# Attention phases of 12 and 14 scores of one head, with two thirds of the q/k projection beside the first 8 groups

## The chip, the cores and the metric

The kernel runs on one core of a Trainium2 chip. The metric is the device time of one execution in microseconds (us). The core has five engines with a queue of instructions each: PE (TensorE, the matrix engine), ACT (ScalarE), DVE (VectorE), POOL (GpSimd) and SP (SyncE, which here only issues DMA transfers). They wait for each other by semaphores. PSUM, where PE writes, has 8 banks of 128 x 512 fp32.

## The reference

The inputs are fp32 with S = 2048 rows, D = 512 columns, H = 32 heads of 16, F = 1792:

```python
x = A_x
g = _sigmoid((x * gate_w).sum(-1, keepdims=True))
# attention
scores = jnp.einsum("bhqd,bhkd->bhqk", q, k) * Dh ** -0.5    # q, k, v from x @ wqkv
a = einsum(softmax(scores), v) @ wo
# token mixing
h = _layernorm(x)
u = _gelu(jnp.einsum("bsd,sf->bdf", h, w1) + b1)             # tanh form
b = (jnp.einsum("bdf,fs->bds", u, w2) + b2)                  # turned back to (b, s, d)
return g * a + (1 - g) * b
```

## The kernel before

fp32 operands are cut in two parts, hi and lo, and a product is three matmuls (hi·hi, hi·lo, lo·hi). P = 128, NB = 512, so a full matmul is 128 rows deep and 512 columns wide; `split` makes a hi part by a copy (ACT or DVE) and a lo part by a subtraction (DVE or POOL). The work is in stages, one after another on PE:

1. x is turned and cut, and v = x·wv is projected; v stays in SBUF.
2. The whole q/k projection: 32 tiles of 12 full matmuls (`products`, L91), alone on PE. Each result is cut and stored in DRAM (`kp_d`, `qp_d`).
3. The first layer (u = gelu(h·w1 + b1)): 14 blocks of 128 columns of w1, 672 full matmuls (L469), in passes of 4 blocks. After a pass `gelu` works its blocks off with ACT and DVE; the last two blocks are worked off where the attention begins.
4. The attention: 32 groups (a pair of heads and half of the queries) of 8 phases, a phase having 8 scores. A score is one matmul 64 rows deep (L926), on one half of the array; on the other half stands, at the same time, a half of a matmul that needs no attention: second layer or output projection (a "dense" matmul, L1053). A phase has 6 or 8 dense ones and scores of both heads. ACT takes the exponentials (L949): two singles of 128 x 512 and three pairs of 128 x 1024, from PSUM into tiles of the pool `pt` (7 buffers of two scores each, 4 tiles in a phase). In 24 of the groups DVE takes one pair instead, by a polynomial (L966 to L990). Behind the 8 scores stand the products with v (A·V) of the phase before (L882, `apply_v`): four matmuls of 17 columns by 256 for each score, in four column strips of the array. DVE adds their bank to the sum of the group (L902). So PE's queue is: 8 scores of phase p, A·V of phase p-1, 8 scores of phase p+1, and so on. The scores and A·V share a ring of 7 banks, by the written table `TURN`; the dense matmuls have the eighth bank.
5. The end: the last group is divided by its sums, and the remaining output matmuls, the adds and the stores of the last 8 row tiles follow.

The stages of the attention are built under a manual schedule: each engine runs its instructions in the order in which the code writes them.

Of the kernel before, what the change touches and what calls it, by code (L numbers as in the profile page):

```python
# [22 lines left out]
P = 128  # L23
# [53 lines left out]
def gated_mix(ctx: ExitStack, tc: tile.TileContext, a_x, a_wqkv, a_wo, b_w1, b_b1, b_w2, b_b2, gate_w, out):  # L77
# [21 lines left out]
    kp_d = [dram.tile([2, P, S], F32, name=f"kp{b}") for b in range(ND)]  # L99

# [13 lines left out]
    v_pool = ctx.enter_context(tc.tile_pool(name="v", bufs=1))  # L114
    v = v_pool.tile([P, NS, H, VC], F32, name="v")

    acc_ctx, wk_ctx, h_ctx, xt_ctx, u_ctx, qk_ctx = (ExitStack() for _ in range(6))
    acc = acc_ctx.enter_context(tc.tile_pool(name="acc", bufs=8, space=PSUM))
    wk = wk_ctx.enter_context(tc.tile_pool(name="wk", bufs=3, side="right"))

    def bank():
        return acc.tile([P, NB], F32, name="acc")


# [3 lines left out]


    order = {f0: [(c + (NS // 2 if f0 + NB >= F else 0)) % NS for c in range(NS)] for f0 in range(0, F, NB)}  # L130
    blocks = [b_w1[c * P : (c + 1) * P, f0 : min(f0 + NB, F)] for f0 in order for c in order[f0]]
    blocks += [
        b_w2[c * P : min(c + 4, NF) * P, t * P : (t + 1) * P].rearrange("(k p) s -> p k s", p=P)
        for t in range(NS)
        for c in range(0, NF, 4)
    ]
    loaded, ready, subs = [], [], []

    def load_weight():
        if blocks:  # L140
            src = blocks.pop(0)
            raw = wk.tile([P, NB], F32, name="w_raw", bufs=4)
            if len(src.shape) == 2:
                raw = raw[:, : src.shape[1]]
                dst = raw
            else:
                raw = raw[:, : src.shape[1] * P]
                dst = raw.rearrange("p (k s) -> p k s", s=P)
            with tc.issue_after(x_load.ins):
                nc.sync.dma_start(dst, src)  # L150
            loaded.append(raw)

    def split_weight(copy=None, sub=None):
        if loaded:
            raw = loaded.pop(0)
            hi = wk.tile([P, NB], F32R, name="w_hi")[:, : raw.shape[1]]
            lo = wk.tile([P, NB], F32R, name="w_lo")[:, : raw.shape[1]]
            subs.append(split(hi, lo, raw, copy or nc.scalar.copy, sub or nc.gpsimd.tensor_tensor))
            ready.append((hi, lo))

    def weight():
        load_weight()
        split_weight()
        return ready.pop(0)
# [14 lines left out]

    def wcols(c0):  # L180
        with tc.issue_after(x_load.ins):
            loaded = load_wcols(c0)
        return split_wcols(*loaded)
# [5 lines left out]
    with tc.tile_pool(name="vp", bufs=1, side="right") as pool:  # L189
# [70 lines left out]

        def v_out(t, ps):
            nc.scalar.copy(v[:, t, :, 0:DH], ps.rearrange("p (h d) -> p h d", d=DH))

        with tc.manual_schedule():
# [64 lines left out]
            for t in range(2, NS):  # L329
# [19 lines left out]
                ps = bank()  # L349
# [4 lines left out]
        pool.tile([P, 40], F32, name="pad")  # L354
        e = pool.tile([P, NS], F32, name="e")
        nc.scalar.activation(e, z, AF.Exp, scale=-1.0)
        nc.vector.tensor_scalar_add(e, e, 1.0)
        nc.vector.reciprocal(g, e)
        nc.vector.tensor_scalar(omg, g, -0.5, 0.5, ALU.mult, ALU.add)
        y, t, w = (pool.tile([P, NS], F32, name=n) for n in "ytw")  # L360
        nc.vector.tensor_scalar_add(w, mv[:, :, 1], EPS)
        nc.scalar.activation(y, w, AF.Sqrt)
        nc.vector.reciprocal(y, y)

        nc.vector.tensor_mul(t, y, y)
        nc.vector.tensor_mul(t, t, w)
        nc.vector.tensor_scalar(t, t, -0.5, 1.5, ALU.mult, ALU.add)
        nc.vector.tensor_mul(rs, y, t)


    NH = NS // 2
    h_hi, h_lo = {}, {}
    AHEAD = 3

    def h_half(lo):
        h_pool = h_ctx.enter_context(tc.tile_pool(name=f"h{lo}", bufs=1))
        hi_t = h_pool.tile([P, NH, D], F32R, name="h_hi")
        lo_t = h_pool.tile([P, NH, D], F32R, name="h_lo")
        for i in range(NH):
            h_hi[lo + i], h_lo[lo + i] = hi_t[:, i, :], lo_t[:, i, :]  # L380

    def ln_load(ln, c, bufs=3):
        xs[c] = ln.tile([P, D], F32, name="x", bufs=bufs)
        nc.sync.dma_start(xs[c], xf[c * P : (c + 1) * P, :])

    def ln_rows(ln, c):
        hf = ln.tile([P, D], F32, name="hf", bufs=2)
        nc.vector.tensor_scalar(hf, xs[c], mv[:, c, 0:1], rs[:, c : c + 1], ALU.subtract, ALU.mult)
        split(h_hi[c], h_lo[c], hf, nc.scalar.copy, nc.vector.tensor_tensor)


    h_half(0)
    bd = h_ctx.enter_context(tc.tile_pool(name="bd", bufs=2))
    bd.tile([P, 56], F32, name="pad", bufs=1)
    with tc.tile_pool(name="ln0", bufs=3, side="right") as ln:

        def project(w, n):
            ps = bank()
            cols = slice(n * NB, (n + 1) * NB)
            hi, lo = w  # L400
            products(ps, [((hi[:, k, :], lo[:, k, :]), (xt_hi[:, k, cols], xt_lo[:, k, cols])) for k in range(ND)])
            return ps
# [837 lines left out]
```

## Time and profile before

| | |
|---|---|
| times of 3 runs | 1267.86, 1268.37, 1269.83 us |
| median | 1268.37 us |
| span of the profiled execution | 1268.3 us |
| busy PE, ACT, DVE, POOL | 99%, 84%, 58%, 18% of the span |
| v and what is ahead of it | 0 to about 50 us |
| q/k projection | about 50 to 139.6 us |
| first layer | 139.6 to 292.1 us |
| attention | 292.1 to 1251.3 us |
| end | 1251.3 to 1268.3 us |

The profiled execution's span is within 0.1 us of the median, so the two are used as one. The busy time of PE is not its useful time: matmuls are pipelined, and a matmul that waits for its turn in the array counts. In rows of the timeline the columns are start and duration in us, engine, line, operation, output <- inputs, shapes, and the count of like instructions that the row takes together. A row of grouped instructions has the count, then the summed time in us and the mean in ns, then the idle time ahead and what ended it.

### The profile page before, as it was taken

The page shows a single profiled execution, that of the slowest core. Times are in us where ns is not written, and L with a number is a line of the kernel's source. Part 1 is how long each engine was busy: PE and PEld are TensorE (multiplying, and loading weights), DVE is VectorE, ACT ScalarE, POOL GpSimd, SP SyncE. Part 2 cuts the span into 40 slices and gives each one's busy share as a digit, 9 for nine tenths or more (in the row PEclk, how much of TensorE's full clock was granted, in tenths as well). Part 3 has the DMA queues.
Part 4 walks back from the last instruction along what each step waited for, and adds up shares of the span by engine and source line. Part 5 has one row for each costly group of instructions (what it writes and reads, how often), then busy time and mean ns, then how long its engine had stood idle before and what let it go on. Part 6 is the DMA issues. An engine that isn't in the chain of part 4 may idle for free.

```text
span 1268.3 us, 33491 instructions
## 1 busy us (share of the span) xinstructions
PE 1259.9 (99%) x13230; PEld 795.6 (63%) x13230; DVE 732.1 (58%) x1342; ACT 1070.1 (84%) x1481; POOL 228.3 (18%) x447
## 2 busy tenths in 40 slices
PE   9999999999999999999999999999999999999998
PEld 7888888886555555555555555555555555555555
DVE  6775362536677666666747656666665662325425
ACT  4444343438999999999999999999999999999994
POOL 4510244553111111111110011111111111100000
PEclk9999999999999999999999999999999999999999
DMA  6787644324223232222444432222222234336622
GB/s 188 218 295 295 226 131 131 98 75 129 73 77 77 75 87 71 77 66 77 128 100 115 117 82 70 69 73 77 76 78 67 77 83 104 95 99 189 156 61 70
DMA packets 108037, 141.10 MB, mean 111 GB/s; under 512 B 20265, under 2 KB 65599, under 8 KB 107872
## 3 DMA queue, kind: packets, MB, share of 16 engines
q1 hardware_dynamic: 107440, 138.09, 38.2%
q8 instruction: 107, 1.75, 0.6%
q10 hardware_dynamic: 432, 0.79, 0.2%
q14 instruction: 58, 0.48, 0.1%
HBM read 102.64 MB, written 36.16 MB: 109 GB/s over the span
## 4 chain that ended last, share of the span: by engine, by line
PE 98%; DMA 0%; DVE 0%; ACT 0%; SPq 0%; issue 0%; ACTq 0%
PE s L882 38%; PE s L926 34%; PE acc L469 12%; PE acc L91 10%; PE dn L1053 4%; PE pa L1124 1%; DMA x<-in_A_x_dram 0%; PE acc L299 0%; PE pa L1133 0%; PE dn L912 0%; PE acc L210 0%; DVE ot L482 0%; SPq L202 0%; DVE base L1152 0%; DVE row L482 0%; ACT row L484 0%
## 5 line engine op out<-in xcount | busy, mean ns | idle before, releaser
L949 ACT ACTIVATE pt<-s 128x1024 f32<-128x1024 f32 (+1 forms) x1256 | 941.4, 945 | 10.6 <-PE s L926 4.5
L926 PE MATMUL s<-qs,ks 64*128 64x512 f32 x2048 | 493.7, 404 | 0.1
L882 PE MATMUL s<-pt,v 128*17 128x256 f32 x8000 | 481.4, 381 | 0.0
L926 PEld LDWEIGHTS s<-qs,ks 64*128 64x128 f32 x2048 | 324.0, 184 | 164.9 <-ACT pt L949 87.8
L902 DVE TENSOR_TENSOR ot<-s,ot 128x256 f32<-128x256 f32 (+2 forms) x431 | 191.5, 444 | 339.6 <-PE s L882 266.2
L882 PEld LDWEIGHTS s<-pt,v 128*17 128x17 f32 x8000 | 209.5, 97 | 233.3 <-ACT pt L949 85.6
L1053 PE MATMUL dn<-u_hi,w_hi 64*128 64x512 f32 x428 | 186.2, 435 | 0.0
L84 POOL TENSOR_TENSOR w_lo<-w_raw,w_hi 128x512 fp32r<-128x512 f32 (+1 forms) x127 | 150.5, 1187 | 170.1 <-ACT w_hi L83 103.9
L1053 PE MATMUL dn<-u_lo,w_hi 64*128 64x512 f32 x430 | 169.4, 394 | 0.0
L1053 PE MATMUL dn<-u_hi,w_lo 64*128 64x512 f32 x430 | 169.1, 393 | 0.0
L1057 POOL MEMSET token<- 1x1 f32 x256 | 25.6, 100 | 779.2 <-PE dn L1053 672.8
L83 ACT CAST w_hi<-w_raw 128x512 fp32r<-128x512 f32 (+1 forms) x67 | 37.8, 569 | 76.6 <-PE acc L469 56.6
L972 DVE SCALAR_TENSOR_TENSOR row<-row,zs 128x512 f32<-128x512 f32 x144 | 99.3, 690 | 4.1
L469 PE MATMUL acc<-h_hi,w_lo 128*128 128x512 f32 x224 | 87.2, 389 | 0.0
L469 PE MATMUL acc<-h_hi,w_hi 128*128 128x512 f32 x224 | 87.1, 389 | 0.0
L469 PE MATMUL acc<-h_lo,w_hi 128*128 128x512 f32 x224 | 87.1, 389 | 0.0
L1053 PEld LDWEIGHTS dn<-u_hi,w_lo 64*128 64x128 f32 x430 | 79.2, 184 | 1.2
L1053 PEld LDWEIGHTS dn<-u_lo,w_hi 64*128 64x128 f32 x430 | 79.4, 185 | 0.8
L1053 PEld LDWEIGHTS dn<-u_hi,w_hi 64*128 64x128 f32 x428 | 78.6, 184 | 1.3
L91 PE MATMUL acc<-xt_hi,wc_hi 128*128 128x512 f32 x128 | 49.8, 389 | 0.0
L91 PE MATMUL acc<-xt_lo,wc_hi 128*128 128x512 f32 x128 | 49.8, 389 | 0.0
L91 PE MATMUL acc<-xt_hi,wc_lo 128*128 128x512 f32 x128 | 49.8, 389 | 0.0
(164 smaller groups left out, 1185.8 us busy)
## 6 DMA issues: line engine op xcount, KB each, us to landing
w_raw<-in_B_w_dram SPq DMA_DIRECT2D x96, 256.0 KB
ks<-kp SPq DMA_DIRECT2D x384, 64.0 KB
qs<-qp SPq DMA_DIRECT2D x256, 64.0 KB
qp<-pc SPq DMA_DIRECT2D x16, 768.0 KB
x<-in_A_x_dram SPq DMA_DIRECT2D x32, 256.0 KB
kp<-pc SPq DMA_DIRECT2D x16, 512.0 KB
w_raw<-in_B_w_dram SPq DMA_DIRECT2D x32, 128.0 KB
bp<-row SPq DMA_DIRECT2D x16, 256.0 KB
```

The source lines that it names most:

```text
L83: copy(hi, src)
L84: return sub(lo, src, hi.bitcast(F32), ALU.subtract)
L91: nc.tensor.matmul(ps, a, b, start=start and n == 0, stop=stop and n == last)
L469: nc.tensor.matmul(p, a, b, start=first and k == 0, stop=last and k == 2)
L882: mm = nc.tensor.matmul(av[32 * j : 32 * j + VC, i * QC : (i + 1) * QC], v[:, c, g % NP * 2 + i, :], pt[:, h * QC : (h + 1) * QC], start=t ...
L902: reads(nc.vector.tensor_tensor(x, y, x, ALU.add), bank)
L926: mm = nc.tensor.matmul(banks[:, bank, :], kt[grp, c * P // SH][rows, c * P % SH : c * P % SH + P], qt[grp][rows, qb * NB : (qb + 1) * NB] ...
L949: act = nc.scalar.activation(dst, banks[:, at[0] : at[-1] + 1, :], AF.Exp, scale=SCALE)
L972: nc.vector.scalar_tensor_tensor(box[1], q or box[1], a, x, ALU.add, ALU.mult)
L1053: mm = nc.tensor.matmul(ps, a[half], b[half], start=first and not second, stop=last and bool(second))
L1057: fence = nc.gpsimd.memset(token, 0.0)
L1124: nc.tensor.matmul(pa[t], a, b, start=i == 0 and t not in LATE, stop=i == len(mms) - 1 and t in LATE)
```

## The change

The changed program has the stages in another order, and its attention another unit of work.

- v is stored to DRAM (`v_d`) and read back for one pair of heads at a time (`load_v`).
- 11 of the 32 tiles of the q/k projection are computed alone (`ALONE`). The other 21 (252 full matmuls) become 504 half matmuls beside the scores of the first 8 groups: pairs 0 to 3 of the heads, both halves of the queries. That is 42 phases of 12 scores, 12 dense matmuls each, and one phase of 8 scores with no dense one.
- The first layer follows, alone, in passes of 3 blocks (the last of 2). The rows of h are made in its first pass, by DVE, ACT, DVE one after another (`ln_rows`).
- The other 24 groups follow: 48 twos of phases of 14 scores (96 phases, all with the second layer beside them), then 8 twos of 12 scores (16 phases, with the output projection of the first 8 row tiles). A two is a phase of the first head of a pair and a phase of its second head with the same dense matmuls, in the two halves. Every score has a dense partner.
- DVE computes no exponential. In a phase of 14 it copies scores 1, 4 and 5 from PSUM into their places in `pt` (`park`, L559), in a phase of 12 scores 2 and 3, and ACT exponentiates these later, in place, from SBUF (L541). The order of ACT's exponentials in a phase is the list `PLANS`.
- Which bank a score gets is no table any more: `take` and `take_beside` choose while the program is built, by estimated times (`SLOT`, `PAIR`, ...). The pool `pt` has 11 buffers in the first 8 groups and 12 in the rest; a phase of 14 fills 7 of them, a phase of 12 fills 6.
- `apply_v` of the phase before still stands behind all scores of a phase, and takes the scores in the order in which their `pt` tiles were opened.
- The end has all 12 output matmuls of each of the last 8 row tiles (9 of them ahead of the last pair of heads); the odd tiles are scaled by ACT and added by POOL.

```diff
+    PLANS = {
+        14: ([(0,), (2,), (3,), (6,), (7,), (8, 9), (10, 11), (12, 13), (5,), (1, 4)], (1, 4, 5)),
+        12: ([(0,), (1,), (4,), (5,), (2, 3), (6, 7), (8, 9), (10, 11)], (2, 3)),
+        8: ([(0,), (1,), (2, 3), (4, 5), (6, 7)], ()),
+    }
...
+        def home(op):
+            nonlocal pt_open, pt_order
+            if op not in homes:
+                pt_order += 1
+                if len(op) == 1 and pt_open is not None:
+                    homes[op] = pt_open[:, 1:2, :]
+                    pt_open = None
+                else:
+                    pt = ptp.tile([P, 2, NB], F32, name="pt")
+                    homes[op] = pt[:, : len(op), :]
+                    if len(op) == 1:
+                        pt_open = pt
+                orders[op] = pt_order
+            return homes[op]
...
+        def park(u):
+            op = next(op for op in ops if u in op)
+            bank = units[u][5]
+            ins = nc.vector.tensor_copy(home(op)[:, op.index(u), :], banks[:, bank, :])
+            reads(ins, bank)
...
+        after(second)
+        apply_v()
+        late = units
...
+        units = sorted(late, key=lambda u: u[6])
...
+    ALONE = 11
...
+        ptp = att_ctx.enter_context(tc.tile_pool(name="pt", bufs=11, reuse_waits="tile"))
...
+        FIRST = 8
...
+        for T in range(ALONE, TILES):
+            box = []
+            run_two(3 * ND, [(qk_step, T, i, box) for i in range(3 * ND)], FIRST)
...
+        passes = [(f0, min(3, NF - f0)) for f0 in range(0, NF, 3)]
...
+        ptp = att_ctx.enter_context(tc.tile_pool(name="pt", bufs=12, reuse_waits="tile"))
...
+        TWO = NF
+        plan = []
+        for t in range(NS):
+            steps = second_layer(t)
+            plan += [steps[n : n + TWO] for n in range(0, 3 * NF, TWO)]
...
+        plan += [project(t) for t in range(NS // 2)]
...
         for _ in range(4):
             for step in gelus:
                 next(step)
+        for step in gelus:
+            list(step)
+        for steps in plan:
+            run_two(len(steps), steps, NG)
```

What the change moves is seen in three places. The first is ACT in one phase of the second layer. A row is the line, the operation, output <- input with the numbers of the buffers (`pt_` tiles in SBUF, `s_` the ring of banks), the shape, the engines whose semaphores it waits for, and a count. Before, a phase with its two singles and three pairs, and the next phase's singles:

```order
L949 ACTIVATE pt_9433<-s_2802 128x512 [waits PE_49] x2
L949 ACTIVATE pt_9442<-s_2802 128x1024 [waits DVE_49,PE_49,Activation_49]
L949 ACTIVATE pt_9448<-s_2802 128x1024 [waits DVE_49,PE_49,Activation_49]
L949 ACTIVATE pt_9454<-s_2802 128x1024 [waits PE_49,Activation_49]
L949 ACTIVATE pt_9479<-s_2802 128x512 [waits PE_49] x2
```

Now a phase of 14:

```order
L547 ACTIVATE pt_11403<-s_673 128x512 [waits PE_49] x2
L547 ACTIVATE pt_11414<-s_673 128x512 [waits PE_49]
L547 ACTIVATE pt_11424<-s_673 128x512 [waits PE_49] x2
L547 ACTIVATE pt_11433<-s_673 128x1024 [waits PE_49]
L547 ACTIVATE pt_11439<-s_673 128x1024 [waits PE_49,Activation_49]
L547 ACTIVATE pt_11446<-s_673 128x1024 [waits PE_49]
L541 ACTIVATE pt_11414<-pt_11414 128x512 [waits DVE_49]
L541 ACTIVATE pt_11406<-pt_11406 128x1024
```

The phase has five singles and five further instructions in place of two and three. Its seven tiles are 11403, 11406, 11414, 11424, 11433, 11439 and 11446. The wait for PE of the last two of them (scores 10 and 11, and 12 and 13) is in the built program not for their scores but for matmuls of A·V: the buffer that 11439 takes is read by the third or fourth score of the A·V that stands behind this phase's scores (in the phase shown the third), the buffer of 11446 by the fifth. The tile of 10 and 11 is the sixth of its phase: 7 tiles of the phase before and the first 5 of this one are all of the pool's 12.

The second place is PE around A·V. Before, the last scores of a phase, the A·V of a phase with four `pt` tiles, and the next phase's first score:

```order
L926 MATMUL s_2802<-qs0_2749,ks0_2751 128x512
L1053 MATMUL dn_9334<-u_hi_1409,w_lo_9100 128x512
L926 MATMUL s_2802<-qs0_2749,ks0_2751 128x512 x2
L882 MATMUL s_2802<-pt_9433,v_88 17x256 x4
L882 MATMUL s_2802<-pt_9442,v_88 17x256 x4
L882 MATMUL s_2802<-pt_9448,v_88 17x256 x4
L882 MATMUL s_2802<-pt_9454,v_88 17x256 x4
L926 MATMUL s_2802<-qs0_2749,ks0_2751 128x512
```

Now, in the same place, with the scores of the phase of which ACT's rows are shown ahead of it:

```order
L577 MATMUL s_673<-qs1_93,ks1_90 128x512
L593 MATMUL dn_11144<-u_hi_4237,w_hi_11094 128x512
L627 MATMUL s_673<-pt_11325,vt_10775 17x256 x2
L627 MATMUL s_673<-pt_11328,vt_10775 17x256 x4
L627 MATMUL s_673<-pt_11336,vt_10775 17x256 x2
L627 MATMUL s_673<-pt_11325,vt_10775 17x256 x2
L627 MATMUL s_673<-pt_11336,vt_10775 17x256 x2
L627 MATMUL s_673<-pt_11346,vt_10775 17x256 x4
L627 MATMUL s_673<-pt_11355,vt_10775 17x256 x4
L627 MATMUL s_673<-pt_11361,vt_10775 17x256 x4
L627 MATMUL s_673<-pt_11368,vt_10775 17x256 x4
L577 MATMUL s_673<-qs0_92,ks2_91 128x512
```

A row of x2 is one score, a row of x4 a pair; the trace counts each of these matmuls as two, so four for a score. The A·V of 14 scores stands in one piece behind 14 scores, and 11325, 11328 and 11336, which hold scores 0 to 5, are read first.

The third place is ACT where the attention begins (before) or begins its second part (now). Before, the gelu of the last two blocks (L479, L484, L488) is woven into the first exponentials:

```order
L83 CAST w_hi<-w_raw 128x512 x2
L479 ACTIVATE ot<-row 128x512
L479 ACTIVATE row<-row 128x512
L484 ACTIVATE ot<-ot 128x512
L484 ACTIVATE row<-row 128x512
L949 ACTIVATE pt<-s 128x512
L488 CAST u_hi<-row 128x512
L949 ACTIVATE pt<-s 128x512
L488 CAST u_hi<-row 128x512
L949 ACTIVATE pt<-s 128x1024 x3
```

Now all of it (L908, L913, L917) stands ahead of them:

```order
L83 CAST w_hi<-w_raw 128x512 x2
L908 ACTIVATE row<-row 128x512
L908 ACTIVATE o_sum<-row 128x512
L913 ACTIVATE row<-row 128x512
L913 ACTIVATE o_sum<-o_sum 128x512
L917 CAST u_hi<-row 128x512 x2
L547 ACTIVATE pt<-s 128x512 x5
L547 ACTIVATE pt<-s 128x1024 x3
```

On PE, 16 full matmuls of the second layer stood ahead of the first score there and 12 behind its phase (L912); now there are none.

1312 lines of the change are left out of this document (674 added, 638 removed), and 3 rows, old and new, of the table TURN.

## The prediction

> **What bounds the kernel now.** I read the head of the page, then the chain that ended last, then the windows by stage, then the waits of PE's loads, and last the timeline of single phases.
>
> ```profile
> PE 1259.9 (99%) x13230; PEld 795.6 (63%) x13230; DVE 732.1 (58%) x1342; ACT 1070.1 (84%) x1481; POOL 228.3 (18%) x447
> PE 98%; DMA 0%; DVE 0%; ACT 0%; SPq 0%; issue 0%; ACTq 0%
> ```
>
> PE carries the chain all the way. The stages (window, length, busy PE, PEld, DVE, ACT, POOL, granted clock, DMA share, GB/s):
>
> ```profile
> 50.30:139.61 89.31, 89.31 (x395) 73.95 (x394) 56.69 (x109) 39.24 (x68) 11.97 (x9) 1.00 0.77 271
> 139.61:292.05 152.44, 152.44 (x674) 126.06 (x672) 67.79 (x86) 61.87 (x110) 75.33 (x63) 1.00 0.44 126
> 292.05:1251.30 959.25, 959.15 (x11878) 549.90 (x11876) 561.97 (x1055) 945.17 (x1263) 113.92 (x351) 1.00 0.33 89
> 1251.30:1268.30 17.00, 10.83 (x80) 7.98 (x80) 8.23 (x16) 1.50 (x3) 1.28 (x1) 0.89 0.36 129
> ```
>
> In the first two PE runs matmuls and ACT is at 44% and 41%. In the attention ACT is busy 945.17 of 959.25 us, as full as PE; its recorded durations overlap, so the true load is found from starts, below. PE waits there for ACT, often and shortly (line waited for, total us, times, longest):
>
> ```profile
> PEld s L926 <- ACT pt L949: 87.8, 207, 0.5
> PEld s L882 <- ACT pt L949: 85.6, 250, 0.4
> ```
>
> So the attention is the stage with two engines near their limit; moving projection matmuls beside scores saves PE time outside it and asks more of the balance inside it.
>
> **PE's price of a phase of 14.** One phase with 8 dense partners, and the A·V of another (start, duration):
>
> ```profile
> 295.76 0.49 PE L926 MATMUL s<-qs,ks 64*128 64x512 f32 x1
> 301.13 0.50 PE L926 MATMUL s<-qs,ks 64*128 64x512 f32 x1
> 301.13 0.50 PE L1053 MATMUL dn<-u_lo,w_hi 64*128 64x512 f32 x1
> 301.47 0.39 PE L926 MATMUL s<-qs,ks 64*128 64x512 f32 x1
> 302.87 0.38 PE L926 MATMUL s<-qs,ks 64*128 64x512 f32 x1
> 303.19 1.92 PE L882 MATMUL s<-pt,v 128*17 128x256 f32 x32
> 698.87 1.06 PE L882 MATMUL s<-pt,v 128*17 128x256 f32 x16
> 699.74 1.05 PE L882 MATMUL s<-pt,v 128*17 128x256 f32 x16
> 700.72 0.50 PE L926 MATMUL s<-qs,ks 64*128 64x512 f32 x1
> ```
>
> A score and its partner start together. The first slot takes 0.34 us, the next six 0.233 each, and A·V begins 0.32 after the last starts. Fourteen slots: 0.34 + 12 x 0.233 + 0.32 = 3.46; the shortest such slots in the trace give 3.43. A·V of 8 scores takes 1.85 from start to next score, of which 4 scores take 0.87: 0.216 a score and 0.12 once. Fourteen: 3.15. PE's own cycle would be 6.58 us, and for 12 scores 5.68. Before, a score with its A·V cost (1251.3 - 295.8) / 2048 = 0.467 us (the first score is the row at 295.76); 6.58 / 14 is 0.470. So PE's price per score hardly changes, while the dense work beside 12 or 14 scores grows.
>
> **ACT's price of it.** Single instructions, by start:
>
> ```profile
> 701.75 0.59 ACT L949 ACTIVATE pt<-s 128x512 f32<-128x512 f32 x1
> 702.23 1.03 ACT L949 ACTIVATE pt<-s 128x1024 f32<-128x1024 f32 x1
> 703.13 1.05 ACT L949 ACTIVATE pt<-s 128x1024 f32<-128x1024 f32 x1
> 704.03 1.06 ACT L949 ACTIVATE pt<-s 128x1024 f32<-128x1024 f32 x1
> 704.94 0.64 ACT L949 ACTIVATE pt<-s 128x512 f32<-128x512 f32 x1
> 705.44 0.64 ACT L949 ACTIVATE pt<-s 128x512 f32<-128x512 f32 x1
> 705.91 1.07 ACT L949 ACTIVATE pt<-s 128x1024 f32<-128x1024 f32 x1
> 297.12 0.58 ACT L949 ACTIVATE pt<-s 128x512 f32<-128x512 f32 x1
> 297.60 0.61 ACT L488 CAST u_hi<-row 128x512 fp32r<-128x512 f32 x1
> 298.10 0.61 ACT L949 ACTIVATE pt<-s 128x512 f32<-128x512 f32 x1
> 297.75 0.50 PE L926 MATMUL s<-qs,ks 64*128 64x512 f32 x1
> ```
>
> A single takes 0.47 to 0.50 us to the next start, a pair 0.90. The cast, which reads SBUF, takes 0.50; no exponential from SBUF is in the trace, so the parked single is put at 0.51 and the parked pair at 0.94 (bounds 0.47 and 0.60 for the single, 0.90 and 1.05 for the pair; the nearest row is the cast, 0.02 to 0.03 above a single from PSUM). A phase of 14: 5 x 0.48 + 3 x 0.905 + 0.51 + 0.94 = 6.57 us. ACT's load would be equal to PE's, with nothing left over. The exponential ends at 297.70, and the score that needed its bank starts at 297.75: 0.05 from release to use.
>
> **The wait that the change adds.** The program's order shows that in a phase of 14 the exponential of scores (10,11), the sixth tile, needs a buffer that is read by the third or fourth score of the A·V standing behind this phase's scores, and (12,13) one that the fifth reads. That A·V starts only when all 14 scores are issued, and score 13 in most phases takes the bank that the exponential of 7 releases. Behind (10,11) on ACT's queue stand (12,13), both parked ones and all of the next phase. The cycle closes on itself:
>
> - A·V starts; its first 4 scores are done after 1.06 (row at 698.87), released 0.05 later: 1.11
> - (10,11) 0.90, (12,13) 0.905, parked 0.51, parked pair 0.94: 3.26
> - next phase: 0, 2, 3 and 6, 0.49 + 3 x 0.478: 1.92
> - 7 to its visible end 0.60, release 0.05: 0.65
> - score 13 to the next A·V's start: 0.32
>
> The sum is 7.26 us. Scores 0 to 7 are there in time: A·V and eight slots end 5.4 us after A·V's start, and exponential 7 begins at 6.3. By the order of the built program 46 of 94 full cycles have score 13 wait for exponential 7 and the rest mostly a neighbour of it, 14 of them an earlier one by about 0.25; mean 7.23. Against 6.58 PE waits 0.65 in each phase, and ACT, with (8,9) done 0.90 after 7, stands about 0.6.
>
> In a phase of 12 (six tiles, 11 or 12 buffers) the same wait is for the second score of A·V, 0.7 us after its start, and ACT comes there later, so it costs nothing; if it cost what it does in a phase of 14 the 57 cycles would give 35 us more. Score 9's bank there waits for the second copy by DVE:
>
> ```profile
> L990 DVE TENSOR_SCALAR zs<-s 128x512 f32<-128x512 f32 x48 | 30.9, 686 | 18.2 <-PE s L926 11.8 <-ACT pt L949 4.1 <-PE dn L1053 2.3
> L902 DVE TENSOR_TENSOR ot<-s,ot 128x256 f32<-128x256 f32 x226 | 95.9, 425 | 308.5 <-PE s L882 240.7 <-ACT pt L949 39.5 <-DMA o<-ot 8.8
> ```
>
> A copy from PSUM is priced by L990, 0.69; the second of two ends 2.34 after the phase's first score against 2.20 needed: 0.14, so 5.82 a phase (bounds 5.68, no wait, and 6.2, the copy behind an L902 of 0.43). DVE's polynomial goes; DVE was at 58%, and its end releases nothing that ends last.
>
> **The sum**, in us of the profiled span (1268.3, the runs' median being 1268.37):
>
> - v: its share ends where the projection's 384 matmuls begin, 139.6 - 384 x 0.2268 = 52.5 (0.2268 is 152.44 / 672). The stores of `v_d` and the loads of K and Q on SP's queue may delay what follows by 0 to 10; I take 0 here, since 11 tiles run meanwhile.
> - 11 tiles alone: 132 x 0.2268 = 29.9, to 82.4.
> - Start of the scores: copy, cut and a table load on ACT ahead of the first exponential,
>
> ```profile
> L484 ACT ACT_TABLE_LOAD x1 | 1.3, 1283 | 0.0
> ```
>
>   1.3 and two instructions of 0.6; seven scores fill the banks meanwhile, and PE loses 4.2 (0 to 8) until it is in step. Then 42 x 5.82 = 244.4, to 331.0.
> - The phase of 8 scores in four slots, with the last A·V, 3.0, and 1.4 of wait for a pair's bank: to 335.4.
> - First layer 152.2 as before, and 6 for the chain that makes h in its first pass (2 to 10): 493.6. A row block of h costs DVE, ACT and DVE:
>
> ```profile
> L388 DVE TENSOR_SCALAR hf<-x,mv,rs 128x512 f32<-128x512 f32 x16 | 9.6, 600 | 16.5 <-DMA x<-in_A_x_dram 16.4
> L83 ACT CAST h_hi<-hf 128x512 fp32r<-128x512 f32 x16 | 9.9, 616 | 11.8 <-DVE hf L388 8.1 <-DMA x<-in_A_x_dram 3.8
> L84 DVE TENSOR_TENSOR h_lo<-hf,h_hi 128x512 fp32r<-128x512 f32 x16 | 16.4, 1025 | 9.8 <-ACT h_hi L83 9.7
> ```
>
>   0.60 + 0.62 + 1.03 = 2.25 against 9 matmuls, 2.04: near enough that the pass may be short by 0.2 for each of 16 blocks, 3 in all, and the first load.
> - Second part: the gelu of the last two blocks now stands wholly ahead of the first exponential on ACT, and no full matmul fills PE:
>
> ```profile
> 292.59 0.63 ACT L479 ACTIVATE ot<-row 128x512 f32<-128x512 f32 x1
> 296.58 0.63 ACT L484 ACTIVATE row<-row 128x512 f32<-128x512 f32 x1 [0.43 <-DVE row L482]
> ```
>
>   From the first L479 to the first exponential (292.59 to 297.12) were 4.5 us; with two casts ahead of it and the last blocks' bias and Square behind the layer's last matmul it is 7.5 (6 to 9) after the layer's end. Seven scores fill the banks and PE waits. ACT then runs the first phase without the new wait (6.57), and the second up to exponential 7; the second phase's A·V starts at 7.5 + 6.57 + 1.92 + 0.65 + 0.32 = 16.95. Then 94 x 7.23 = 679.6, one step to phases of 12 of 6.3, 15 x 5.82 = 87.3, and the last A·V's 5.6: 795.7 in all, to 1289.3.
> - End: 96 full matmuls, 21.8, and 48 small ones for the last pair, of which 16 took 1.20: 25 us, to 1314.3. The last tile goes over ACT and POOL instead of DVE and the stores follow:
>
> ```profile
> 1254.23 1.20 PE L1133 MATMUL pa<-wq,hi 16*128 16x512 f32 x16
> 1256.02 0.69 ACT L1146 ACTIVATE res<-pa,g 128x512 f32<-128x512 f32 x1 [1.80 <-PE pa L1133]
> 1262.17 0.75 DVE L1152 SCALAR_TENSOR_TENSOR base<-pa,g,base 128x512 f32<-128x512 f32 x1 [0.19 <-PE pa L1124]
> 1256.78 1.28 POOL L1147 TENSOR_TENSOR base<-res,base 128x512 f32<-128x512 f32 x1 [8.85 <-ACT res L1146]
> ```
>
>   From 1262.92 to the span's end were 5.38; with about 0.5 until ACT begins, its 0.69 and POOL's 1.28 the tail is 7.85.
>
> 1314.3 + 7.85 = 1322 us, 4.2% above before. Where the gain went: 252 projection matmuls and 28 full ones of the second layer leave PE's own time (64 us), and 61 us of waits come in the phases of 14, with the starts and ends (4, 6, 10 and 15) and the phases' own length making up the rest.
>
> **The rivals.** *Slots run free, faster.* If the buffer is there when ACT comes (its wait being already met, or A·V's first scores ending sooner), a phase of 14 takes 6.58 to 6.6, and the sum falls by 94 x 0.63 = 60 to 1262, 0.5% faster. It decides at (1268.4 - 1322) / 94 = 0.57 below 7.23, a phase of 6.66. For it: nothing in the trace shows that wait, and ACT and PE at 6.57 and 6.58 allow it. Against it: A·V follows score 13, and score 13 follows exponential 7, by the order. Chance 0.11, with 1245 to 1280 about it.
>
> *Half of the wait.* If exponentials are shorter from one head's scores, or score 13's bank is another, a phase takes 6.8 to 6.9 and the time is near 1285 (1268 to 1300). Chance 0.12.
>
> *The clock falls.* The granted clock is 1.00 in the three long stages, where the loads of PE wait for ACT 0.3 to 0.4 us at a time, and 0.89 in the end, where it idles 6 of 17 us. If 0.65 us in every phase brings 0.89, the parts of the cycle that PE runs (1.43 of 7.23) grow by 12%, 0.17 a phase, 16 us: 1338. Chance 0.07. The Trainium skill, "TensorE: Matmul & The Clock Gate", section "A second HAM failure mode: psum-queue depth-cycling", says that PE idling briefly and often as it goes round PSUM banks can make the clock swing between half and full. By that rule with half the clock throughout, those 1.43 us would double and the sum be 1322 + 94 x 1.43 = 1456. The trace before has 457 such waits of PE for ACT at a granted clock of 1.00, which speaks against it here.
>
> *Late transfers.* v, K and Q come from DRAM at the start of the first part; if the queue of SP holds them 10 us, and the first layer's loads too, the time is 1335 to 1340. Chance 0.06.
>
> **How the numbers follow.** The main case has the rest, 0.64, at 1300 to 1345 by its bounds (first part 9 less or 22 more, starts 4 to 8 either way, parked exponentials 0.13 a phase). The time is its middle, 1322. The range takes in half of the wait at 1285 and the late transfers: 1285 to 1345. It leaves out the free slots and the slow clock's far end. From no change a measurement of this kernel can tell about 0.2%, so 1265.8 to 1270.9. Of the free slots' 0.11 I give 0.08 to faster, 0.02 to same and 0.01 to slower, of the half wait's 0.12 0.01 to same, and all else is slower: 0.08, 0.03 and 0.89.
>
> **What would show it.** In the profile after: ACT's exponential of (10,11) waiting about 0.6 us for PE's A·V once in each of 96 phases; A·V starts 7.2 us apart in the phases of 14 and 5.8 in those of 12; PE's busy share of the second part falling; the granted clock 1.00. I am wrong if phases of 14 are under 6.7 us, if PE's waits for ACT in them sum to under 20 us, or if the first part's phases are over 6.2.

## The result: slower by 11%, and the profile after

The changed kernel takes 1410.53 us (median of 4 runs, 1407.69 to 1411.08) against 1268.13 for the one before, a ratio of 1.1113 (95% interval 1.1097 to 1.1129). The forecast had the sign, and the place of one of the losses, but not the size: 1322, with a range to 1345. The profiled execution has a span of 1409.2 us. From its page, busy time and the chain that ended last:

```profile
PE 1342.4 (95%) x13446; PEld 801.3 (57%) x13446; DVE 627.6 (45%) x1124; ACT 1103.1 (78%) x1641; POOL 251.5 (18%) x386
PE 30%; ACT 26%; issue 3%; POOL 0%; ACTq 0%; POOLq 0%
PE s L577 19%; ACT pt L547 17%; PE s L627 10%; ACT pt L541 10%; PE dn L593 1%; POOL base L1196 0%; ACTq L547 0%; POOLq L960 0%; POOLq L1196 0%; POOL token L598 0%; POOLq L598 0%
```

Before, PE alone carried the chain. Now it goes to and fro between PE's scores (L577), ACT's exponentials (L547, and L541 from SBUF) and A·V (L627); the shares in the second row add up to 59% of the span, and the page names nothing for the rest. By stage (window, length, busy PE, PEld, DVE, ACT, POOL, granted clock, DMA share, GB/s):

```profile
60.61:123.45 62.84, 44.52 (x230) 33.59 (x228) 22.68 (x49) 30.45 (x47) 6.58 (x7) 0.80 0.72 207
123.45:366.69 243.24, 240.78 (x2885) 134.97 (x2882) 128.73 (x226) 230.90 (x321) 38.47 (x70) 1.00 0.34 105
376.82:552.78 175.96, 165.21 (x672) 128.24 (x672) 78.18 (x98) 67.20 (x131) 81.16 (x81) 0.95 0.42 120
552.78:573.23 20.45, 13.81 (x113) 8.60 (x112) 10.56 (x18) 15.95 (x25) 3.17 (x6) 0.75 0.14 41
573.23:1275.43 702.20, 692.45 (x7900) 375.31 (x7896) 277.02 (x520) 635.07 (x941) 88.17 (x175) 1.00 0.30 82
1288.19:1365.55 77.36, 77.36 (x942) 44.19 (x938) 47.76 (x83) 75.08 (x105) 2.21 (x15) 1.00 0.56 165
1374.40:1409.20 34.80, 25.52 (x144) 19.89 (x142) 9.21 (x17) 3.49 (x6) 5.10 (x4) 0.91 0.21 75
```

The rows are: the 11 tiles alone and the first two phases; the next 40 phases of 12 (6.08 us each); the first layer; the first two phases of 14; the other 94 (702.20 / 94 = 7.47 each); 13 of the last phases of 12 (5.95 each); the end. PE counts as busy in almost all of the 702 us, though by its own price 94 phases are 619 (94 x 6.58): its records leave hardly a gap while it waits for a bank. So PE's busy share doesn't show the loss, and the waits do:

```profile
PEld s L577 <- ACT pt L547: 187.9, 510, 7.7
ACT pt L547 <- PE s L627: 67.4, 95, 1.7
```

(Line waited for, total us, times, longest, over the whole execution.) PE's loads for scores wait for ACT, and ACT's exponential waits for PE's A·V, 95 times and 0.71 us each. The second is the wait that the prediction put into the cycle. One cycle of it, ACT's rows first:

```profile
1004.09 1.03 ACT L547 ACTIVATE pt<-s 128x1024 f32<-128x1024 f32 x1 [0.72 <-PE s L627]
1005.01 1.02 ACT L547 ACTIVATE pt<-s 128x1024 f32<-128x1024 f32 x1
1005.91 0.64 ACT L541 ACTIVATE pt<-pt 128x512 f32<-128x512 f32 x1
1006.43 1.06 ACT L541 ACTIVATE pt<-pt 128x1024 f32<-128x1024 f32 x1
1007.38 0.60 ACT L547 ACTIVATE pt<-s 128x512 f32<-128x512 f32 x1
1008.81 1.11 ACT L547 ACTIVATE pt<-s 128x512 f32<-128x512 f32 x2
1009.29 0.64 ACT L547 ACTIVATE pt<-s 128x512 f32<-128x512 f32 x1
```

```profile
1002.94 0.63 PE L627 MATMUL s<-pt,vt 128*17 128x256 f32 x8
1009.50 0.50 PE L577 MATMUL s<-qs,ks 64*128 64x512 f32 x1
1009.84 0.62 PE L577 MATMUL s<-qs,ks 64*128 64x512 f32 x2
1010.40 0.84 PE L627 MATMUL s<-pt,vt 128*17 128x256 f32 x12
```

A·V starts at 1002.94, (10,11) begins 1.15 us later with the end of its wait, (12,13), the parked single and the parked pair follow without a gap, 0 of the next phase at 1007.38, 6 at 1008.81 (its row takes 6 and 7 together; the row after it is 7 alone), 7 at 1009.29, and the next A·V at 1010.40: 7.46 us.

### The profile page after: what moved, and what is told of

It is laid out like the page before. It is cut to its first block, busy times and chain, and to the rows that moved or that the text cites. A ratio compares the mean times of both kernels' runs of the same rounds, so it can differ in the third digit from the quotient of the medians.

```text
span 1409.2 us, 33193 instructions
## 1 busy us (share of the span) xinstructions
PE 1342.4 (95%) x13446; PEld 801.3 (57%) x13446; DVE 627.6 (45%) x1124; ACT 1103.1 (78%) x1641; POOL 251.5 (18%) x386
## 4 chain that ended last, share of the span: by engine, by line
PE 30%; ACT 26%; issue 3%; POOL 0%; ACTq 0%; POOLq 0%
PE s L577 19%; ACT pt L547 17%; PE s L627 10%; ACT pt L541 10%; PE dn L593 1%; POOL base L1196 0%; ACTq L547 0%; POOLq L960 0%; POOLq L1196 0%; POOL token L598 0%; POOLq L598 0%
## 5 line engine op out<-in xcount | busy, mean ns | idle before, releaser
L547 ACT ACTIVATE pt<-s 128x512 f32<-128x512 f32 (+1 forms) x1179 | 808.6, 783 | 80.9 <-PE s L627 67.4
L577 PE MATMUL s<-qs,ks 64*128 64x512 f32 x2048 | 613.7, 423 | 37.5 <-ACT pt L547 15.5
L577 PEld LDWEIGHTS s<-qs,ks 64*128 64x128 f32 x2048 | 352.0, 186 | 290.5 <-ACT pt L547 187.9
L627 PE MATMUL s<-pt,vt 128*17 128x256 f32 x8192 | 471.8, 380 | 0.0
L627 PEld LDWEIGHTS s<-pt,vt 128*17 128x17 f32 x8192 | 225.7, 97 | 220.6 <-issue 42.5
L559 DVE COPY pt<-s 128x512 f32<-128x512 f32 x404 | 257.9, 686 | 34.6 <-PE s L577 21.6
L541 ACT ACTIVATE pt<-pt 128x512 f32<-128x512 f32 (+1 forms) x250 | 214.4, 901 | 8.1 <-DVE pt L559 8.0
L84 POOL TENSOR_TENSOR w_lo<-w_raw,w_hi 128x384 fp32r<-128x384 f32 (+2 forms) x144 | 154.8, 1080 | 120.2 <-ACT w_hi L83 93.7
L949 PE MATMUL s<-h,w_hi 128*128 128x512 f32 x448 | 147.6, 406 | 14.2 <-ACT w_hi L83 8.2
L949 PEld LDWEIGHTS s<-h,w_hi 128*128 128x128 f32 x448 | 86.3, 193 | 41.1 <-ACT w_hi L83 8.6
L949 PE MATMUL s<-h,w_lo 128*128 128x512 f32 x224 | 90.1, 402 | 0.0
```

Source lines behind the costliest of these rows:

```text
L84: return sub(lo, src, hi.bitcast(F32), ALU.subtract)
L541: act = nc.scalar.activation(dst, dst, AF.Exp, scale=SCALE)
L547: act = nc.scalar.activation(dst, banks[:, at[0] : at[-1] + 1, :], AF.Exp, scale=SCALE)
L559: ins = nc.vector.tensor_copy(home(op)[:, op.index(u), :], banks[:, bank, :])
L577: mm = nc.tensor.matmul(banks[:, bank, :], kt[2 * grp + c * P // SH][rows, c * P % SH : c * P % SH + P], qt[grp][rows, qb * NB : (qb + 1) ...
L627: mm = nc.tensor.matmul(av[32 * j : 32 * j + VC, at : at + QC], vt[grp][:, i, c, :], pt[:, h * QC : (h + 1) * QC], start=m == 0, stop=m == ...
```

## The experiments

Where no ratio is given, a time is that of single executions. Ahead of the first edit in a program, times still differ: in the eight edited kernels that change nothing ahead of the 11 tiles, and in which PE ran at its usual length, these began at 55.9 to 60.0 us, against 60.6 in the changed kernel. A difference of up to 5 us in a single time is therefore read from stages, not from totals.

**Fourteen buffers, and thirteen.**

```diff
-        ptp = att_ctx.enter_context(tc.tile_pool(name="pt", bufs=12, reuse_waits="tile"))
+        ptp = att_ctx.enter_context(tc.tile_pool(name="pt", bufs=14, reuse_waits="tile"))
...
```

Four tiles of the end take the memory of `o_parts` that are dead by then, to make room. The second run has 13.

> The only edit: the pool pt of the second part has 14 buffers instead of 12 (four tiles of the end share memory that is dead by then). Theory A (the wait for a pt buffer closes the cycle): the waits of ACT for A-V, 67.4 us in 95 times, go; a phase of 14 falls from 7.47 us to 6.7-6.8, where ACT's 6.57 and PE's 6.58 bound it, and the time from 1410 to 1335-1350. Rival B (the ring of 7 banks binds; a score that waits for an exponential would wait as long without the buffer wait): a phase stays over 7.2 and the time over 1385.

> 13 buffers instead of 12. Theory A: only scores 12 and 13 now wait for A-V's first scores; 1.15 + 0.92 + 0.52 + 0.95 + 1.43 + 1.59 = 6.56 for that cycle, which is no more than ACT's own 6.57, so one buffer buys all of what two buy: 6.7-6.9 a phase, 1335-1355. If A-V's release counts for each tile (a wait that shrinks in steps), a phase lies halfway, near 7.1, and the time near 1375.

Measured: 1338.80 and 1340.82 us. The windows of the same 94 phases, with 14 buffers and with 13:

```profile
567.88:1204.03 636.15, 635.10 (x7901) 378.12 (x7897) 275.01 (x520) 631.64 (x942) 88.60 (x175) 1.00 0.33 90
```

```profile
569.97:1205.91 635.94, 635.01 (x7901) 377.93 (x7897) 275.74 (x520) 633.69 (x942) 88.55 (x175) 1.00 0.33 90
```

6.77 us a phase instead of 7.47, and no wait of ACT for A·V is left in the list of waits. 66 of the 72 us are in this window. Theory A holds, and one buffer of 4 KB a partition does what two do: when only (12,13) wait for the first scores of A·V, the cycle through that wait is, by the sum in the second expectation, 6.56 us and no longer than ACT's own load of 6.57; that the wait is gone is measured, the 6.56 is not. ACT is now busy 631.64 of 636.15, so the balance of ACT and PE sets the phase.

**The first layer.** Two edits in one run: h two blocks ahead, and the loads for the second part spread, one piece at every second row block.

```diff
-                    if c + 1 < NS:
-                        ln_rows(c + 1, nc.scalar.copy)
+                    for k in (1, 2) if c == 0 else (c + 2,):
+                        if k < NS:
+                            ln_rows(k, nc.scalar.copy)
...
-                load_ahead(pos, NG)
+                for m in range(16, 19):
+                    pieces.extend((load_k, m, [i]) for i in range(2))
+                for grp in (8, 9):
+                    pieces.extend((load_q, grp, [i]) for i in range(2))
+                    pieces.append((load_v, grp))
...
+                if pieces and c % 2:
+                    what, *args = pieces.pop(0)
+                    what(*args)
```

What they were aimed at, from the trace of the changed kernel: SP's queue and, behind it, ACT.

```profile
448.32 8.29 SPq L467 DMA_DIRECT2D ks<-kp  x18
456.66 3.68 SPq L467 DMA_DIRECT2D qs<-qp  x8
460.38 0.42 SPq L486 DMA_DIRECT2D vt<-v_d  x1
460.85 3.70 SPq L467 DMA_DIRECT2D qs<-qp  x8
464.59 0.42 SPq L486 DMA_DIRECT2D vt<-v_d  x1
465.11 1.83 SPq L849 DMA_DIRECT2D w_raw<-in_B_w_dram  x4
```

```profile
468.54 1.09 ACT L83 CAST w_hi<-w_raw 128x384 fp32r<-128x384 f32 x2 [12.25 <-DMA w_raw<-in_B_w_dram]
```

The next loads of w1 stand behind 18 + 8 + 1 + 8 + 1 = 36 issues of some 0.46 us, from 448.3 to 465.1; ACT waits 12.25 us for them and PE 8.16 (8.55 from the start of one matmul to the start of the next).

> In the first layer h is made two row blocks ahead instead of one, and the 36 DMA issues of K, Q and V for the second part are spread over two passes instead of standing in one piece ahead of w1's loads on SP's queue. Theory A: the first pass falls from 2.53 us a row block to 2.06 (14 x 0.47 = 6.6 us), the gap of 8.55 us in the third pass and the 13 slow matmuls behind it (2.6 us) go: 17 to 19 us less, about 1392. Rival B (the DMA engines, not the queue's order, are what the third pass waits for): the gap stays, spread out, and only 6 to 7 us are won, about 1403.

Measured: 1397.13 us. The layer's window:

```profile
375.27:539.29 164.02, 162.10 (x672) 126.73 (x672) 77.56 (x98) 67.31 (x131) 81.24 (x81) 0.98 0.44 128
```

11.9 us less, and nearly all of that is the spread: no gap is left in the third pass, so the order of the queue was the cause, not the DMA engines. The lead of two blocks gave next to nothing: the first pass stays at 2.53 us a block. DVE's rows in it show why:

```profile
396.32 1.24 DVE L869 TENSOR_SCALAR hf<-x,mv,rs 128x512 f32<-128x512 f32 x1
398.24 0.69 DVE L84 TENSOR_TENSOR h<-hf,h 128x512 fp32r<-128x512 f32 x1 [0.69 <-ACT h L83]
398.85 1.24 DVE L869 TENSOR_SCALAR hf<-x,mv,rs 128x512 f32<-128x512 f32 x1
```

From one L869 to the next are 2.53 us: the row is normalised, DVE stands until ACT has cast it, subtracts, and only then begins the next row. A lead moves this loop forward and doesn't shorten it. My theory for this half was wrong, and the time missed its 1392.

**h in two steps.** The spread loads, and on DVE the row of block c+2 ahead of the subtraction of block c+1.

```diff
-            split(h[c][:, 0, :], h[c][:, 1, :], hf, copy, nc.vector.tensor_tensor)
+            return lambda: split(h[c][:, 0, :], h[c][:, 1, :], hf, copy, nc.vector.tensor_tensor)
...
+                    if c + 2 < NS:
+                        cut.append(ln_rows(c + 2, nc.scalar.copy))
+                    if cut:
+                        cut.pop(0)()
...
```

> As the first-layer experiment, but on DVE the normalised row of the block after next stands ahead of the lo part of the next block, so that DVE no longer waits for ACT's cast in between. Theory A (DVE, ACT, DVE in one serial loop of 2.53 us set the first pass, whatever the lead): a row block falls to 2.06-2.1, 14 x 0.45 = 6 us less than the first-layer experiment's 1397: 1390-1392. Rival B (POOL's w_lo, 1.10 us and started late, or x's loads set it): it stays at 2.5 and the time at 1396-1398.

Measured: 1390.37 us. The layer:

```profile
371.48:531.82 160.34, 158.60 (x673) 126.74 (x673) 77.11 (x98) 67.64 (x131) 81.61 (x81) 0.99 0.45 131
```

The gaps at every block are gone; 3.7 us are won in the stage, where 6 were expected, because two gaps of 0.97 and 1.44 us between the starts of matmuls near the fifth block take their place. In this execution the layer also begins 3.8 us earlier (371.48 against 375.27), which the edit doesn't touch; without that the total would lie above theory A's range. In the run without this edit, PE's gap in each block, 0.17 us, was ended by POOL's `w_lo`, so POOL stood as a rival. POOL is as busy as before (81.61 against 81.24 us), and the gaps are gone all the same: the serial loop was the cause.

**Parks 1 and 3.**

```diff
-        12: ([(0,), (1,), (4,), (5,), (2, 3), (6, 7), (8, 9), (10, 11)], (2, 3)),
+        12: ([(0,), (2,), (4,), (5,), (1, 3), (6, 7), (8, 9), (10, 11)], (1, 3)),
```

> In phases of 12 DVE parks scores 1 and 3 instead of 2 and 3. Theory A (score 9's bank waits for the second copy's end, 2.3 us after the phase's first score): the second copy ends 0.23 us sooner, the stall and the slow restart behind it go, a phase falls from 5.95 to 5.68-5.75 in 57 phases: 12 to 15 us less, about 1397. Rival B (ACT's exponentials bind, 5.55 of load and the wait at a phase's first score): a phase stays at 5.9 or over, no change beyond 3 us.

Measured: 1400.86 us. 13 of the last phases of 12:

```profile
1279.82:1355.18 75.36, 75.36 (x941) 44.29 (x937) 47.55 (x83) 74.80 (x105) 2.22 (x15) 1.00 0.60 170
```

5.80 us instead of 5.95, between the two theories: the second copy did hold PE, and behind it ACT, busy 74.80 of 75.36, now sets the phase a little above PE's 5.68. 57 times 0.15 is 8.6 of the 9.7 us; the theory's 12 to 15 were missed.

**v stored late.**

```diff
-                if t == NS // 2 + 1:
-                    nc.sync.dma_start(v_half(0), v_src(0))
...
+            nc.sync.dma_start(v_half(0), v_src(0))
             nc.sync.dma_start(v_half(1), v_src(1))
```

> The first half of v is stored to DRAM behind v's last product instead of before the last loads of x. Theory A (that store of 2176 KB on SP's queue and the DMA engines makes the last four loads of x take 8.99 us where 2.04 were needed before, and PE waits): v ends 6 to 8 us sooner, at 53-55 instead of 60.6, and the first A-V comes 2 to 8 us sooner, the rest of the program unchanged: 1402-1408. Rival B (x's loads are late for another reason): v ends at 60 as it does now and the time stays at 1407-1412.

Measured: 1401.65 us. The last four loads of x on SP's queue, in the changed kernel and with this edit:

```profile
40.33 8.99 SPq L197 DMA_DIRECT2D xb<-in_A_x_dram  x4
```

```profile
38.45 2.43 SPq L197 DMA_DIRECT2D xb<-in_A_x_dram  x4
```

v's products end at 53.2 instead of 60.6, and the first A·V comes at 112.4 instead of 120.7. Theory A holds as to the cause: in every execution with the early store and PE at its usual length these four loads take 8.68 to 9.01 us, in the three with the late store 2.04 to 2.43. The price is less even. v's products end at 55.9 to 60.6 us with the early store, so it cost 3 to 7 us, all on PE's path. In the changed kernel PE waited 3.37 us for the last row block, and the matmuls behind came 0.43 us apart; in the execution with 55.9 the waits were 1.54 and 1.10 us, and the matmuls stayed 0.23 apart.

**The weights cut later.**

```diff
-                cuts[T + 1] = bring_wcols(T // NQ + 2)
+                cuts[T + 5] = bring_wcols(T // NQ + 2)
...
```

> The only edit: the next weights of the q/k projection are cut by DVE four tiles later (and the third block as a job beside the first scores), so that DVE's queue does not stand at their cast while the transfer is under way. Theory A (DVE's two waits of 10.0 and 14.3 us for wc_raw hold back the parts behind them, and with these ACT's buffers and the first exponential): the first exponential comes at 99-104 instead of 107, the first A-V at 111-117 instead of 120.7, 1402-1407. Rival B (the stores of q and k, and the three buffers behind them, set the start by themselves): the first A-V stays at 118-121, no change beyond 3 us.

Measured: 1401.64 us. Where the changed kernel's start stands, first on ACT, then on DVE and behind it on PE:

```profile
105.13 0.62 ACT L83 CAST pc<-qraw 128x512 fp32r<-128x512 f32 x1 [8.88 <-DMA qp<-pc]
111.42 0.43 DVE L83 CAST wc_hi<-wc_raw 128x512 fp32r<-128x512 f32 x1 [14.33 <-DMA wc_raw<-in_A_wqkv_dram]
112.95 1.28 DVE L559 COPY pt<-s 128x512 f32<-128x512 f32 x2
113.69 0.79 PE L577 MATMUL s<-qs,ks 64*128 64x512 f32 x1 [5.18 <-DVE pt L559]
```

The first exponential comes behind the cast at 105.13, and the copies of the first phase's parked scores stand on DVE's queue behind the cast of the weights. The waits between 60 and 125 us, in the changed kernel and with this edit:

```profile
DVE wc_hi L83 <- DMA wc_raw<-in_A_wqkv_dram: 26.4, 3, 14.3
ACT pc L83 <- DMA qp<-pc: 15.6, 3, 8.9
```

```profile
ACT pc L83 <- DMA qp<-pc: 15.5, 4, 8.8
DVE wc_hi L83 <- DMA wc_raw<-in_A_wqkv_dram: 4.1, 1, 4.1
```

DVE's wait shrinks from 26.4 to 4.1 us and the first A·V comes 7.9 us sooner (112.9; 7.2 counted from the start of the 11 tiles), though the first exponential only 2.4 (104.7), since ACT still waits 8.8 us for a store ahead of it. So two queues stood at the start: DVE for weights, ACT for a free buffer of `pc`.

**q and k stored from ACT's queue.**

```diff
-            qk_parts(T, raw, True)()
+            if behind:
+                behind.pop()(nc.scalar)
+            behind.append(qk_parts(T, raw, True))
...
```

With the queue, one thing more is moved: the loads of K, Q and v for the first part are issued one tile later.

> In the 11 tiles computed alone, each tile's parts of q and k are stored from ACT's queue, one tile later, instead of from SP's, where they stand behind the loads of K, Q and v. Theory A (ACT's cast of the last tile, ahead of the first exponential, waits 8.9 us for a store of T = 7 that SP issues behind 30 loads): the first exponential comes at 95-100 instead of 107, the first A-V at 109-115 instead of 120.7, the time 1398-1405. Rival B (the DMA engines' throughput, 71% busy there, is what the start waits for): the first A-V stays within 3 us of 120.7 and the time within 4 of 1409.

This run tells nothing by itself. Its 4318.18 us are from an execution in which PE was slow from end to end:

```profile
L577 PE MATMUL s<-qs,ks 64*128 64x512 f32 x2048 | 1708.3, 1078 | 8.6 <-ACT pt L547 8.6
```

A score takes 1078 ns there against 423, and the other matmuls of 512 columns 1065 to 1099, in every stage. Those of v come 0.84 us apart, where the other runs have 0.23:

```profile
101.18 1.16 PE L91 MATMUL acc<-wv_hi,xt_hi 128*128 128x512 f32 x1
102.02 1.00 PE L91 MATMUL acc<-wv_lo,xt_hi 128*128 128x512 f32 x1
```

It is PE alone: ACT's exponentials (766 ns against 783) and DVE's copies (692 against 686) keep their length. The cause is not in the kernel's edit, since the same edit is in the next run without it; what it was stays open. The granted clock is recorded as 1.00, and 0.84 us is twice the 0.43 at which such matmuls follow one another where it is recorded as 0.50.

**Five edits together**: 14 buffers, parks 1 and 3, spread loads, h in two steps, stores on ACT's queue.

> 14 buffers, parks 1 and 3 in phases of 12, spread loads, h in two steps, and the stores of q and k on ACT's queue, together. Theory A (the causes are separate places on PE's path and their times add): 71 + 9.5 + 11 + 6 + 5 to 10 off 1410.5: 1303-1308, still 2.8% above the kernel before, because the phases' own time, the 96 matmuls at the end, and the starts of the two parts stay. Rival B (a fix gives time back elsewhere, by DMA or the banks): over 1315.

Measured: 1314.98 us (ratio to before 1.0351, 1.0332 to 1.0369). The phases and the layer gave what they gave alone (6.74 and 5.80 us; the layer 160.8). The start missed: the first score comes at 89.7 instead of 97.4, the first exponential still at 107.5, because DVE's wait for weights was still there. The result missed theory A's range and lies at rival B's edge for that reason, not because a gain was given back elsewhere.

**gelu later.**

```diff
-        for _ in range(4):
+        for _ in range(2):
             for step in gelus:
                 next(step)
-        for step in gelus:
-            list(step)
+        for _ in range(STEPS - 2):
+            for step in gelus:
+                jobs.append((two, 0.7, lambda step=step: next(step)))
```

> The only edit: of the gelu of the last two blocks only the bias and the square stand ahead of the second part; the other steps come behind the scores of its first phases. Theory A (the exponentials wait for this chain on ACT): the second phase's A-V comes 10-12 us after the layer's last matmul instead of 17.6, 5 to 7 us less in all: 1402-1406. Rival B (the steps take ACT's time in the first phases, where ACT is full anyway, and the gain is given back): less than 3 us.

Measured: 1404.70 us. The second phase's A·V comes 12.2 us after the start of the layer's last matmul instead of 17.6, but the next two cycles take 8.51 and 9.12 us, and from the second part's first score to the last A·V only 3.0 us are won (813.0 against 816.0). The rest of the total is the start and the layer, which the edit doesn't touch; only with it does the total lie in theory A's range. So 2.5 of the 5.5 us gained at first are given back while ACT works off the steps, and what is left is at the edge of rival B's "less than 3 us", below theory A's 5 to 7.

**Eight edits, and seven.** The five, with v stored late, the cut later and gelu later; then the same with the stores of q and k back on SP's queue, and the loads of K, Q and v back at their tiles.

> All edits so far: 14 buffers, parks 1 and 3, spread loads, h in two steps, stores of q and k on ACT's queue, v stored late, cut later, gelu later. Theory A (places that add): 1315 less 8 for v, 2 to 5 for the cut, 5 to 7 for the gelu: 1295-1301. Rival B (the start is bound by the DMA engines, which move the same bytes in any order): v and the cut give nothing together, 1306-1310.

> As the run of eight edits, but with the stores of q and k on SP's queue again. Theory A (SP's order still holds the stores back behind the loads of K, Q and v): 4 to 8 us over the eight edits. Rival B (with DVE's wait gone the stores leave in time): within 2 us of them.

Measured: 1298.34 us (ratio to before 1.0229, 1.0212 to 1.0246) and 1302.48 (1.0269, 1.0252 to 1.0286). With eight edits the first exponential comes at 89.1 instead of 107.1 and the first A·V at 101.7; with seven at 96.5 and 105.1. So SP's order, with the loads a tile earlier, costs 4 us more even without DVE's wait. 112 of the 142 us are found, and none of these versions beats the kernel before. Of the 29 us that remain, 22 stand in the end: from the start of the last A·V to the last instruction, with eight edits and in the kernel before:

```profile
1255.70:1296.20 40.50, 31.14 (x242) 23.01 (x240) 12.40 (x24) 6.77 (x10) 5.20 (x5) 0.90 0.24 81
```

```profile
1249.82:1268.30 18.48, 12.31 (x108) 8.64 (x100) 9.61 (x19) 1.65 (x4) 1.28 (x1) 0.90 0.33 118
```

The end has 96 full matmuls that no score accompanies, where before 32 were left; that this share can be moved beside scores was not tried.

## Why the prediction missed, by its own steps

The span missed by 1409.2 - 1322 = 87 us. By stage, forecast and measured, in us:

| step of the sum | forecast | measured | missed by |
|---|---|---|---|
| v ends | 52.5 | 60.6 | 8.1 |
| 11 tiles, start of the scores, first two phases (29.9 + 4.2 + 2 x 5.82) | 45.7 | 62.8 | 17.1 |
| 40 phases of 12 | 232.8 | 243.2 | 10.4 |
| phase of 8 and its A·V | 4.4 | 6.6 | 2.2 |
| first layer | 158.2 | 179.5 | 21.3 |
| second part up to the second A·V | 16.95 | 17.3 (first scores in) | 0.4 |
| 94 phases of 14 | 679.6 | 702.2 | 22.6 |
| phases of 12 behind them, last A·V | 99.2 | 102.1 | 2.9 |
| end and tail | 32.85 | 34.8 | 2.0 |

The fourth column adds up to 87, of which 69 lie in three places: the start (8.1 and 17.1), the phases of 14 and the first layer.

*The wait for a pt buffer* was right, place, number of times and all: 95 waits, gone with one more buffer. Fourteen of the 94 cycles are shorter by 0.2 us or more, about as many as the prediction had. Its term was 0.24 us short in each phase. The prediction let score 13 wait for exponential 7; in the cycle shown score 11 waits for exponential 6, and after that wait the slots take 0.34 and 0.23, so that three slots and A·V's start follow at 1.59 us from exponential 6 where 1.45 was put. A stalled slot costs its refill too: 0.34 instead of 0.23, as the first slot behind A·V does. The same 0.11 is in the phases of 12 (5.95 against 5.82), and eight of the first 40 phases are 0.5 to 0.9 longer, which was not in the sum: there PE waits for DVE's copies.

*The start* is where the step failed: "I take 0 here, since 11 tiles run meanwhile". PE came 25 us late (8.1 and 17.1 in the table), by places that the order shows: the store of v ahead of x's last loads, the loads of K, Q and v ahead of the stores of q and k, and the weights' cut on DVE ahead of parts of q and k. The eight edits together bring the first A·V forward by 19.0 us (120.7 to 101.7). The other 6 are not shown to be transfers: PE still waits 5.41 us there for its load of q, and matmuls behind long waits come at half the granted clock. The rival of late transfers named SP's queue but gave it 13 to 18 us and 0.06, as if it excluded the main case; it came on top of it.

*The first layer*: "6 for the chain that makes h (2 to 10)". The chain of 0.60, 0.62 and 1.03 was taken as throughput (2.25 against 2.04 us a block). It is a serial loop on DVE's queue, with 1.24 instead of 0.60 for the normalised row, and came to 2.53. The gap of 8.55 us behind 36 DMA issues was missed altogether: a block of loads that the change moves on SP's queue was not priced there. The half of the 6 that stood for the first load was about right: PE waits 3.46 us ahead of the first matmul.

*The end* and the order of the stages were as forecast. *The second part's start* (16.95 against 17.3) agrees partly by luck. ACT's first row of exponentials, the second phase's first, and the granted clock between them:

```profile
559.70 1.57 ACT L547 ACTIVATE pt<-s 128x512 f32<-128x512 f32 x3
567.47 3.48 ACT L547 ACTIVATE pt<-s 128x512 f32<-128x512 f32 x6
556.57:566.79 10.22, 6.42 (x27) 4.42 (x29) 5.40 (x9) 7.91 (x13) 1.37 (x2) 0.50 0.00 0
```

The first exponential comes 6.9 us after the layer's end, where 7.5 was put, and the first phase then takes ACT 7.77 us instead of 6.57, with PE at half the clock. The rival of free slots would have had 1262, and without the buffer wait the kernel is at 1339: had that wait been absent, the sign would still have been slower, by the start, the first layer and phases of 6.77 instead of 6.58 us.

*The clock*: the forecast's rival of 0.89 throughout did not come. The granted clock is 1.00 in the 702 us in which PE pauses in every phase, and low only around the long waits and in the end. In the Trainium skill, "TensorE: Matmul & The Clock Gate", the section "A second HAM failure mode: psum-queue depth-cycling" has short pauses between groups of matmuls bring the clock down; no run here shows that for pauses of this length.

## What to carry to other kernels

Count the buffers of a pool against all that is written before the first reader runs: 7 tiles a phase, and a reader that stands behind the next phase's scores, need more than 12, and one buffer too few closed a cycle through two engines for 0.7 us in every phase. Price each queue as a queue: what stands behind a block of DMA issues, a big store or a cast that waits for a transfer is delayed with it, on SP as well as on DVE and ACT. When single edits are laid together, a start with several waits gives its time back in full only when the last of them is gone.

## What the runs showed of the hardware

After PE had waited 3.46 us ahead of the first layer, its next matmuls of 512 columns came 0.43 us apart (the first two gaps were longer), and from the thirteenth on 0.23 to 0.27:

```profile
376.82 1.52 PE L949 MATMUL s<-h,w_hi 128*128 128x512 f32 x2 [3.46 <-DVE h L83]
378.13 0.63 PE L949 MATMUL s<-h,w_lo 128*128 128x512 f32 x1
```

The granted clock is 0.50 from 375.66 to 382.47 us. The same follows the wait of 8.16 us in the third pass. Each of the two cost about 2.5 us on top of itself (12 times 0.20). The price isn't fixed: ahead of the first layer PE waited 2.94 to 3.63 us in the kernels of all the experiments in which it ran at its usual length, and between 7 and 14 slow matmuls followed, in two of them only behind the first three. The Trainium skill, "TensorE: Matmul & The Clock Gate", section "Part 1: The HAM clock gate (the "warmup" mystery)", has the clock at half after an idle window of some 3.4 us and full again after as long a busy one. The trace agrees with the factor of about two and with a wait of 3.46 us as enough for it; the slow stretch here is 5.6 us (376.82 to 382.40). In the run with parks 1 and 3 a wait of 2.94 us was enough too, less than the section's idle window. The prediction had left this price out of every start and every wait.
